# A convolution feeding a multiplicative FFN: loading x in two halves, issuing row transposes as soon as their rows are stored, and transposing block 2 on TensorE

## The chip, the cores and the metric

The kernel runs on one core of a Trainium2 chip. The metric is the device time of one launch in microseconds. The kernel before took 584.01, 588.37 and 587.26 us in three runs, median 587.26. One execution was profiled: it took 585.55 us, and its span, from the first to the last instruction of the program, is 583.8 us. Durations below are from that execution.

## The reference

What is computed, cut to what matters:

```
x: (8, 3904, 192) float32      weight: (8 heads, 7 taps)
w1, w2: (192, 1024)   w3: (1024, 1024)   w_out: (1024, 192)

w   = softmax(weight, axis=-1)
# causal convolution over the sequence; head h owns channels 24h .. 24h+23
c[b, s, h, :] = sum_k w[h, k] * x[b, s - 6 + k, h, :]        (zeros before s = 0)
c   = c.reshape(31232, 192)
out = ((c @ w1) * (c @ w2)) @ w3 @ w_out
```

## The kernel before

The 31232 tokens are two halves of TS = 15616 tokens (NS = 2, the index r). Both halves are worked on together: each takes 64 of the 128 partitions. Everything after the convolution goes in rounds R = 0 to 30 of CH = 512 tokens of each half (the last has 256).

**Convolution.** The tokens are cut into windows of 58 (64 rows of x, the first 6 of them overlap). Windows come in blocks of sizes 10, 10, 10, 30, 32 and then five times 36 (`SIZES`, L52); block b starts at token `tok(FIRST[b])`, which is 0, 580, 1160, 1740, 3480, 5296, 7384, 9432, 11520, 13568. `load_x` (L91) loads a block's x into one or two `xb` tiles (two halves of the block's windows, `halves_of`) with POOL's DMA queue, converting to bf16. There are six `xb` buffers. `conv` (L231) multiplies the windows with a band matrix made of the weights, head by head, into PSUM, and copies the result to the tile `convo` (two buffers). `store` (L262) writes `convo` with SP's DMA queue to a DRAM tensor `rows`, one row per token.

**Transposition.** `first_product` needs channels on partitions. `xT` is a ring of 2048 tokens (four rounds), in three parts of 128 partitions. `transposes(R)` (L301) fills a round of it with three DMA transposes from `rows`, on SP's queue. `pe_transposes(b)` (L286) does it without DRAM: 15 transposes on TensorE from `convo` into PSUM, and three copies into `xT`, two on DVE and one on ACT. In the kernel before, blocks 0 and 1 take that way; block 2 goes through `rows`, with the last windows of block 1 (`store(1, 19)`, from token 1102).

**The products.** `first_product(R)` (L327) runs eight steps `ft`; each has 12 matmuls for `pa` and `pb`, ACT's copy of `pa` to `asb` and DVE's product into `abT`. `second_product(R, r)` (L352) multiplies `abT` with `W_sb` = w3 @ w_out; ACT copies the result to `osb` and SP's queue stores it. It lags two rounds (`LAG`). PSUM is four tiles of two banks, shared by all of these.

**Order.** It is written out by hand (`manual_schedule`): every engine does its instructions in the order in which the code issues them.

- POOL's opening: x of block 0, the masks (L152), four DMAs of `load_first` (L133), the identity (L158, L159), the loads of `wn[0]` and the two halves of `wn[2]` (L163 to L165), the products of half of the band matrix (L203, `band_taps(1, ...)`), then `wn[1]` (L407), and blocks 1 and 2 of x. DVE makes the other half of the products at the same time as POOL's earlier work, sums them into `Aband` (L211), and copies it to the other partitions (L214).
- Rounds 0, 1 and 2 of `first_product` have the convolutions of blocks 1, 2 and 3 between their steps (L433 to L443); in round 1 after step 0: the rest of block 2's convolution, its store, and `transposes(2, 1152)`. After round 2's step 5: block 3's store, `transposes(3)` and `transposes(4)`. Then comes w3 @ w_out on TensorE.
- The loop over R (L462) does, in each round: `first_product(R)` (from R = 3), `second_product(R - 2)` for both halves, `conv` of one to three heads of the next block by the table `plan`, `store` of a block after its last head, and `transposes(R + 2)` last. Block 4 is stored in round 4, block 5 in round 7, block 6 in 11, block 7 in 15, block 8 in 19, block 9 in 23. In the round of a block's first head, `load_x` of the next block is issued whole (L473); the DMA waits until the convolution that read the buffers before is done.

So SP's queue holds, in this order, the outputs of round R - 2, a block's store if there is one, and the transposes for round R + 2.

Of the kernel before, what the change touches and what calls it, by code (L numbers as in the profile page):

```python
# [10 lines left out]
BF16 = mybir.dt.bfloat16  # L11
# [6 lines left out]
def kernel(  # L18
# [10 lines left out]
    nc = tc.nc  # L29
# [6 lines left out]
    PAD = K - 1  # L36

    NS = 2
    TS = B * S // NS
    CH = 512  # L40
    NR = -(-TS // CH)
    RING = 4 * CH
    LAG = 2
    Q = 64
    ST = Q - PAD
# [4 lines left out]
    SIZES = [10, 10, 10, 30, 32] + [36] * 5  # L50
    assert sum(SIZES) == NWIN
    NB = len(SIZES)  # L52
    FIRST = [sum(SIZES[:b]) for b in range(NB)]
# [4 lines left out]
    def tok(i):  # L58
        return (i // WB) * S + (i % WB) * ST

    const = ctx.enter_context(tc.tile_pool(name="const", bufs=1))
# [12 lines left out]
    def slot(shape, dtype, name):  # L74
        return stage.tile(shape, dtype, tag="slot", bufs=5, name=name)
# [4 lines left out]
    def halves_of(b):  # L80
        n = SIZES[b] // 2
        return [(FIRST[b], 2 * n)] if 2 * n <= MAXN else [(FIRST[b], n), (FIRST[b] + n, n)]

    x_rows = x.rearrange("b s d -> (b s) d")
    xb_of, zero_rows = {}, {}

    def x_spans(r, i, m):
        return bass.AP(tensor=x.tensor, offset=(r * TS + tok(i) - PAD) * D,
                       ap=[[D, Q], [ST * D, m], [1, D]])

    def load_x(b):  # L91
        tiles = []
        zeros_of = zero_rows[b] = []
        for i0, n in halves_of(b):
            xb = work.tile([128, n, D], BF16, tag="xb", bufs=6, name="xb")
            w = 0
            if i0 == 0:
                nc.gpsimd.memset(xb[:, 0, :], 0.0)
                for r in range(NS):
                    nc.gpsimd.dma_start(out=xb[Q * r:Q * r + Q, 1:n, :], in_=x_spans(r, 1, n - 1))  # L100
                w = n
            while w < n:
                i = i0 + w
                m = min(n - w, WB - i % WB)
                at_end = i + m == NWIN
                if at_end:
                    m -= 1
                if m:
                    for r in range(NS):
                        nc.gpsimd.dma_start(out=xb[Q * r:Q * r + Q, w:w + m, :],  # L110
                                            in_=x_spans(r, i, m))
                if i % WB == 0:
                    zeros_of += [(xb, 0, w), (xb, 1, w)]
                w += m
                if at_end:
                    nc.gpsimd.memset(xb[Q:128, w, :], 0.0)
                    t = tok(NWIN - 1) - PAD
                    nc.gpsimd.dma_start(out=xb[0:Q, w, :], in_=x_rows[t:t + Q, :])
                    nc.gpsimd.dma_start(out=xb[Q:Q + PAD + LAST, w, :],
                                        in_=x_rows[TS + t:TS + t + PAD + LAST, :])  # L120
                    w += 1
            tiles.append(xb)
        if len(tiles) == 1:
            xb_of[b] = [(tiles[0], 0), (tiles[0], SIZES[b] // 2)]
        else:
            xb_of[b] = [(tiles[0], 0), (tiles[1], 0)]


    def load_first():
        xb = xb_of[0][0][0]  # L130
        for r in range(NS):
            for p0, p1 in ((PAD, PAD + 48), (PAD + 48, Q)):
                nc.gpsimd.dma_start(  # L133
                    out=xb[Q * r + p0:Q * r + p1, 0, :],
                    in_=x_rows[r * TS + p0 - PAD:r * TS + p1 - PAD, :])

    wall = const.tile([128, H, K], FP32)
    nc.scalar.dma_start(out=wall, in_=weight.partition_broadcast(128))
    load_x(0)

    tiny = const.tile([128, 1], FP32)
# [9 lines left out]
    for m, base in ((cmask, 0), (lmask, -Q)):  # L151
        nc.gpsimd.affine_select(  # L152
            out=m, in_=ones.unsqueeze(2).to_broadcast([128, K, Q]),
# [1 line left out]
            fill=0.0, base=base, channel_multiplier=1)  # L155
    nc.vector.tensor_copy(out=cmask[Q:128], in_=lmask[Q:128])
    load_first()
    ident = const.tile([128, 128], BF16)  # L158
    make_identity(nc, ident)  # L159

    wn = [const.tile([128, DFF], BF16, name=f"wn{k}", tag=f"wn{k}") for k in range(3)]
    wsw = [const.tile([128, DFF], BF16, name=f"ws{k}", tag=f"ws{k}") for k in range(3)]
    nc.gpsimd.dma_start(out=wn[0], in_=moe_w1[0:128, :])  # L163
    nc.gpsimd.dma_start(out=wn[2][0:Q], in_=moe_w1[128:192, :])
    nc.gpsimd.dma_start(out=wn[2][Q:128], in_=moe_w2[128:192, :])  # L165

    def warm(n):
        t = banks("warm")
# [11 lines left out]
        out=wall, in0=wall, in1=wmax.unsqueeze(2).to_broadcast([128, H, K]), op=ALU.subtract)  # L180
# [3 lines left out]
    for r in range(NS):  # L184
        ps = slice(Q * r, Q * r + Q)
        nc.vector.tensor_tensor(
            out=wsb[ps],
# [13 lines left out]
    def band_taps(g, engine):  # L201
        cprod_of[g] = slot([128, 2, K, Q], FP32, "cprod")
        engine.tensor_tensor(  # L203
            out=cprod_of[g],
            in0=cmask.unsqueeze(1).to_broadcast([128, 2, K, Q]),
            in1=wsb[:, g].unsqueeze(3).to_broadcast([128, 2, K, Q]),
            op=ALU.mult)
# [23 lines left out]
    def conv(b, h0, nh, evict=None):  # L231
# [27 lines left out]
        if h0 + nh == H:  # L259
            del xb_of[b]  # L260

    def store(b, first=0):  # L262
        n = SIZES[b] // 2
        convo = convo_of[b]
        for c in range(2):
            w = 0
            while w < n:
                i = FIRST[b] + c * n + w
                if i < first:
                    w += 1  # L270
                    continue
                left = WB - 1 - i % WB
                src = convo[Q * c:Q * c + ST, w:w + max(1, min(n - w, left))]
                src = src.rearrange("s w k r g -> s w (k r g)")
                j0 = tok(i)
                if left == 0:
                    nc.sync.dma_start(out=rows[j0:j0 + LAST, :], in_=src[0:LAST, 0, :])
                    w += 1
                    continue
                m = min(n - w, left)  # L280
                dst = rows[j0:j0 + ST * m, :].rearrange("(w s) c -> s w c", s=ST)
                for s0, s1 in ((0, 48), (48, ST)):
                    nc.sync.dma_start(out=dst[s0:s1], in_=src[s0:s1])
                w += m
# [16 lines left out]
    def transposes(R, first=0):  # L301
        t0, t1 = max(R * CH, first), min((R + 1) * CH, TS)
        a = t0 % RING
        for k in range(NP):
            nc.sync.dma_start_transpose(  # L305
                out=xT[k][:, a:a + t1 - t0], in_=rows[t0:t1, k * 128:(k + 1) * 128])
# [78 lines left out]
    def w3_transpose(jt):  # L385
        w3b = w3b_of.pop(jt)
        tps = banks_bf16("w3ps")
        for gt in range(JT):
            nc.tensor.transpose(out=tps[:, gt, :], in_=w3b[:, gt * 128:(gt + 1) * 128],  # L389
                                identity=ident)  # L390
        w3T_of[jt] = stage.tile([128, JT, 128], BF16, tag="w3T", bufs=3, name="w3T")
        nc.vector.tensor_copy(out=w3T_of[jt], in_=tps[:, 0:JT, :])  # L392
# [11 lines left out]

    band_taps(0, nc.vector)
    band_taps(1, nc.gpsimd)
    nc.gpsimd.dma_start(out=wn[1], in_=moe_w2[0:128, :])  # L407
    for b in (1, 2):
        load_x(b)
    band_sum(0)  # L410
# [8 lines left out]
    for k in (0, 2, 1):  # L419
        swap_w(k, 1, (P, A))  # L420
    load_x(3)
    load_wo()
    for jt in range(JT):
# [3 lines left out]
    def seq(*fs):  # L427
        def run():
            for f, *a in fs:
                f(*a)  # L430
        return run

    first_product(0, {  # L433
        3: seq((conv, 1, 0, 4)),
        5: seq((conv, 1, 4, 4)),
        7: seq((pe_transposes, 1), (store, 1, 19), (conv, 2, 0, 4))})
    first_product(1, {
        0: seq((conv, 2, 4, 4), (store, 2), (transposes, 2, 1152)),
        7: seq((conv, 3, 0, 1), (conv, 3, 1, 1))})
    first_product(2, {  # L440
        1: seq((conv, 3, 2, 1), (conv, 3, 3, 1)),
        3: seq((conv, 3, 4, 1), (conv, 3, 5, 1)),
        5: seq((conv, 3, 6, 1), (conv, 3, 7, 1), (store, 3), (transposes, 3), (transposes, 4))})  # L443

    w3_transpose(0)
    w3_transpose(1)
# [7 lines left out]
    R = LAG  # L454
    for b in range(PROLOGUE_BLOCKS, NB):
        last = tok(FIRST[b]) // CH - (2 if b == PROLOGUE_BLOCKS else 3)
        hs, n = list(range(H)), last - R + 1
        for j in range(n):
            plan[R + j] = [(b, hs.pop(0)) for _ in range(-(-len(hs) // (n - j)))]
        R = last + 1  # L460

    for R in range(LAG, NR + LAG):  # L462
        if LAG < R < NR:
            first_product(R)
        for r in range(NS):
            second_product(R - LAG, r)
        heads = plan.get(R, [])
        if heads and heads[0][1] == 0:
            b = heads[0][0]
            for xb, r, w in zero_rows.pop(b):  # L470
                nc.gpsimd.memset(xb[Q * r:Q * r + PAD, w, :], 0.0)
            if b + 1 < NB:
                load_x(b + 1)  # L473
        for j, (b, h) in enumerate(heads):
            conv(b, h, 1, (V,) if j < 2 else (A,))
        if heads and heads[-1][1] == H - 1:
            store(b)
        if LAG < R < NR - 2:
            transposes(R + 2)


# [28 lines left out]
```

## Time and profile before

| what | us |
|---|---|
| median of three runs (584.01 to 588.37) | 587.26 |
| the profiled execution | 585.55 |
| its span | 583.8 |
| TensorE (PE) busy | 535.8 (92%) |
| VectorE (DVE) busy | 358.4 (61%) |
| ScalarE (ACT) busy | 319.6 (55%) |
| GpSimd (POOL) busy | 50.1 (9%) |
| DMA packets of SP's queue, share of 16 engines' span | 35.0% |
| DMA packets of POOL's queue, share of 16 engines' span | 24.8% |

The busy time of PE counts a matmul longer when TensorE's clock is granted at half speed, so a busy PE isn't PE at its best. How the clock stands is shown by the granted clock, and by the time of six matmuls of `first_product`, which is 0.65 us at the full clock and 1.28 us at half. "SPq" and "POOLq" are the DMA queues of SP and POOL: a time there is that of issuing, not of the transfer.

### The profile page before, as it was taken

The page shows a single profiled execution, that of the slowest core. Times are in us where ns is not written, and L with a number is a line of the kernel's source. Part 1 is how long each engine was busy: PE and PEld are TensorE (multiplying, and loading weights), DVE is VectorE, ACT ScalarE, POOL GpSimd, SP SyncE. Part 2 cuts the span into 40 slices and gives each one's busy share as a digit, 9 for nine tenths or more (in the row PEclk, how much of TensorE's full clock was granted, in tenths as well). Part 3 has the DMA queues.
Part 4 walks back from the last instruction along what each step waited for, and adds up shares of the span by engine and source line. Part 5 has one row for each costly group of instructions (what it writes and reads, how often), then busy time and mean ns, then how long its engine had stood idle before and what let it go on. Part 6 is the DMA issues. An engine that isn't in the chain of part 4 may idle for free.

```text
span 583.8 us, 12613 instructions
## 1 busy us (share of the span) xinstructions
PE 535.8 (92%) x5425; PEld 343.8 (59%) x5425; DVE 358.4 (61%) x330; ACT 319.6 (55%) x360; POOL 50.1 (9%) x80
## 2 busy tenths in 40 slices
PE   6894888996999689997899989999999999999997
PEld 2441484664566446665366666656666666666687
DVE  6671636664666466665566666876666666666550
ACT  2872735653565255553455545666555556666642
POOL 9632300020003000030000000000000000000000
PEclk8996998999899989999799999999999999999999
DMA  6999995459346953349533272235532262333214
GB/s 92 182 215 177 113 169 93 82 107 195 79 83 124 180 92 82 82 83 204 106 83 83 77 170 42 70 82 147 125 83 64 62 155 75 82 82 83 69 56 136
DMA packets 131830, 63.72 MB, mean 109 GB/s; under 512 B 84620, under 2 KB 130366, under 8 KB 131774
## 3 DMA queue, kind: packets, MB, share of 16 engines
q1 hardware_dynamic: 93470, 46.26, 35.0%
q0 software_dynamic: 38160, 16.63, 24.8%
q8 instruction: 42, 0.69, 0.5%
q14 instruction: 14, 0.11, 0.1%
q10 hardware_dynamic: 144, 0.03, 0.0%
HBM read 33.28 MB, written 35.13 MB: 117 GB/s over the span
## 4 chain that ended last, share of the span: by engine, by line
PE 80%; DMA 12%; ACT 3%; POOL 2%; DVE 2%; SPq 1%; issue 1%; ACTq 0%; POOLq 0%
PE pa L340 27%; PE pb L340 27%; PE ops L358 25%; DMA xT<-rows 10%; PE cps L247 1%; ACT asb L346 1%; DMA rows<-convo 1%; DVE abT L347 1%; DMA wn<-in_moe_w_dram 1%; SPq L305 1%; ACT convo L257 0%; POOL xb L133 0%; ACT osb L363 0%; POOL xb L100 0%; ACT ws L319 0%
## 5 line engine op out<-in xcount | busy, mean ns | idle before, releaser
L347 DVE TENSOR_TENSOR abT<-asb,pb 128x1024 bf16<-128x1024 bf16 (+1 forms) x248 | 298.0, 1203 | 106.4 <-ACT asb L346 51.8
L346 ACT CAST asb<-pa 128x1024 bf16<-128x1024 f32 (+1 forms) x248 | 247.5, 999 | 112.4 <-PE pa L340 111.7
L340 PE MATMUL pa<-xT,wn 64*128 64x512 bf16 (+1 forms) x744 | 206.6, 381 | 24.2 <-DMA xT<-rows 21.5
L340 PE MATMUL pa<-xT,ws 64*128 64x512 bf16 (+1 forms) x744 | 206.7, 381 | 11.3 <-DMA xT<-rows 10.6
L340 PEld LDWEIGHTS <-wn 64*128 64x128 bf16 x1488 | 138.8, 95 | 119.9 <-issue 26.3
L340 PE MATMUL pb<-xT,wn 64*128 64x512 bf16 (+1 forms) x744 | 206.2, 380 | 0.7 <-DVE abT L347 0.7
L340 PE MATMUL pb<-xT,ws 64*128 64x512 bf16 (+1 forms) x744 | 199.8, 381 | 0.0
L340 PEld LDWEIGHTS <-ws 64*128 64x128 bf16 x1488 | 130.9, 95 | 82.0 <-issue 19.3
L358 PEld LDWEIGHTS <-abT 128*128 128x128 bf16 x1952 | 159.6, 98 | 11.7 <-issue 11.7
L358 PE MATMUL ops<-W_sb,abT 128*128 128x192 bf16 x1952 | 166.1, 246 | 0.0
L363 ACT COPY osb<-ops 128x768 f32<-128x768 f32 (+1 forms) x62 | 48.9, 789 | 127.6 <-PE ops L358 127.6
L257 DVE CAST convo<-cps 128x864 bf16<-128x864 f32 (+4 forms) x53 | 44.9, 894 | 93.2 <-PE cps L247 80.7
L110 POOL DMA_DIRECT2D xb<-in_x_dram x38 | 29.9, 809 | 175.6 <-issue 103.1
L247 PE MATMUL cps<-xb,Aband 64*64 64x432 bf16 (+3 forms) x320 | 18.9, 322 | 5.2 <-DVE Aband L211 2.9
L257 ACT CAST convo<-cps 128x640 bf16<-128x640 f32 (+8 forms) x29 | 15.3, 581 | 3.5 <-PE cps L247 2.9
L247 PEld LDWEIGHTS <-Aband 64*64 64x64 bf16 x320 | 6.4, 110 | 14.5 <-issue 8.2
L398 PE MATMUL wps<-wo_b,w3T 128*128 128x192 bf16 x64 | 6.6, 246 | 1.3 <-DVE w3T L392 1.2
L170 PE MATMUL warm<-zeros 128*128 128x512 bf16 x19 | 6.5, 507 | 1.3 <-DVE zeros L144 1.3
L392 DVE COPY w3T<-w3ps 128x1024 bf16<-128x1024 bf16 x8 | 5.4, 689 | 2.9 <-PE w3ps L389 2.9
L400 ACT CAST W_sb<-wps 128x192 bf16<-128x192 f32 x8 | 2.6, 320 | 8.1 <-PE wps L398 8.1
L398 PEld LDWEIGHTS <-w3T 128*128 128x128 bf16 x64 | 5.1, 98 | 1.7 <-DVE w3T L392 1.7
L383 POOL DMA_DIRECT2D w3b<-in_moe_w_dram x8 | 4.3, 558 | 7.9 <-DMA xb<-in_x_dram 6.7
(47 smaller groups left out, 50.8 us busy)
## 6 DMA issues: line engine op xcount, KB each, us to landing
out_dram<-osb SPq DMA_DIRECT2D x60, 384.0 KB
xb<-in_x_dram POOLq DMA_DIRECT2D x14, 432.0 KB, 12.6
rows<-convo SPq DMA_DIRECT2D x7, 648.0 KB
w3b<-in_moe_w_dram POOLq DMA_DIRECT2D x8, 256.0 KB, 12.3
xb<-in_x_dram POOLq DMA_DIRECT2D x6, 240.0 KB, 7.2
xb<-in_x_dram POOLq DMA_DIRECT2D x4, 360.0 KB, 9.3
xT<-rows SPq DMA_TRANSPOSE x87
xb<-in_x_dram POOLq DMA_DIRECT2D x6, 192.0 KB, 10.3
```

The source lines that it names most:

```text
L110: nc.gpsimd.dma_start(out=xb[Q * r:Q * r + Q, w:w + m, :], in_=x_spans(r, i, m))
L170: nc.tensor.matmul(t[:, j % 2, :], zeros[:, 0:128], zeros, start=True, stop=True)
L247: nc.tensor.matmul(view(slice(Q * c, Q * c + Q), r)[:, :, j * G:(j + 1) * G], band_of(h, r), xb[Q * r:Q * r + Q, w0:w0 + n, h * G:(h + 1) ...
L257: f[e % len(f)](out=dst, in_=src[:, :, :, o:o + m])
L305: nc.sync.dma_start_transpose(out=xT[k][:, a:a + t1 - t0], in_=rows[t0:t1, k * 128:(k + 1) * 128])
L340: nc.tensor.matmul(p[:, r, 0:N], w_of(i, k, r)[rs, ft * 128:(ft + 1) * 128], xT[k][rs, r0:r0 + N], start=(k == 0), stop=(k == NP - 1))
L346: nc.scalar.copy(out=asb[:, :, 0:N], in_=pa[:, :, 0:N])
L347: nc.vector.tensor_tensor(out=ab[:, ft, :, 0:N], in0=asb[:, :, 0:N], in1=pb[:, :, 0:N], op=ALU.mult)
L358: nc.tensor.matmul(ops[:, g // 2, (g % 2) * D:(g % 2) * D + D], ab[:, jt, r, g * 128:(g + 1) * 128], W_sb[:, jt, :], start=(jt == 0), stop ...
L363: nc.scalar.copy(out=osb.rearrange("p (a g) d -> p a (g d)", g=2), in_=ops[:, 0:ng // 2, 0:2 * D])
L392: nc.vector.tensor_copy(out=w3T_of[jt], in_=tps[:, 0:JT, :])
L398: nc.tensor.matmul(wps[:, 0, 0:D], w3T[:, gt, :], wo_b[:, gt, :], start=(gt == 0), stop=(gt == JT - 1))
```

## The change

1. `load_x` takes the halves that it is to load. In the loop, half 0 of the next block is issued in the round of a block's first heads, half 1 in the round after. In the opening both are loaded as before.
2. `transposes` in the loop are issued as far as rows are stored (`stored`), up to three rounds ahead (`sent`): `transposes(5)` in round 2, 6 and 7 in round 4 behind the store of block 4, 8 in round 5, and from there `transposes(R + 3)` in round R.
3. Block 2 is transposed on TensorE, after step 2 of round 1. Of its rows only windows 26 to 29 are stored (`transposes(3)` needs them), and `store(1, 19)` and `transposes(2, 1152)` are gone.
4. POOL's first work: `load_first` is two DMAs of 58 partitions, where it was four of 48 and 10. The identity and the loads of `wn[2]` come after POOL's products for the band matrix, in the order `wn[2]` (two DMAs), `wn[1]`, identity.

```diff
-    def load_x(b):
-        tiles = []
-        zeros_of = zero_rows[b] = []
-        for i0, n in halves_of(b):
+    def load_x(b, parts=(0, 1)):
+        tiles = xb_of.setdefault(b, [])
+        zeros_of = zero_rows.setdefault(b, [])
+        for i0, n in [v for e, v in enumerate(halves_of(b)) if e in parts]:
...
-            for p0, p1 in ((PAD, PAD + 48), (PAD + 48, Q)):
-                nc.gpsimd.dma_start(
-                    out=xb[Q * r + p0:Q * r + p1, 0, :],
-                    in_=x_rows[r * TS + p0 - PAD:r * TS + p1 - PAD, :])
+            nc.gpsimd.dma_start(out=xb[Q * r + PAD:Q * r + Q, 0, :],
+                                in_=x_rows[r * TS:r * TS + ST, :])
...
     load_first()
-    ident = const.tile([128, 128], BF16)
-    make_identity(nc, ident)
...
     nc.gpsimd.dma_start(out=wn[0], in_=moe_w1[0:128, :])
-    nc.gpsimd.dma_start(out=wn[2][0:Q], in_=moe_w1[128:192, :])
-    nc.gpsimd.dma_start(out=wn[2][Q:128], in_=moe_w2[128:192, :])
...
+    stored, sent = [0], [3]
+
     def store(b, first=0):
+        stored[0] = tok(FIRST[b] + SIZES[b]) if b + 1 < NB else TS
...
     band_taps(1, nc.gpsimd)
+    nc.gpsimd.dma_start(out=wn[2][0:Q], in_=moe_w1[128:192, :])
+    nc.gpsimd.dma_start(out=wn[2][Q:128], in_=moe_w2[128:192, :])
     nc.gpsimd.dma_start(out=wn[1], in_=moe_w2[0:128, :])
+    ident = const.tile([128, 128], BF16)
+    make_identity(nc, ident)
...
-        7: seq((pe_transposes, 1), (store, 1, 19), (conv, 2, 0, 4))})
+        7: seq((pe_transposes, 1), (conv, 2, 0, 4))})
     first_product(1, {
-        0: seq((conv, 2, 4, 4), (store, 2), (transposes, 2, 1152)),
+        0: seq((conv, 2, 4, 4)),
+        2: seq((pe_transposes, 2), (store, 2, 26)),
...
+    sent[0] = 5
...
+    done_of = {}
     for R in range(LAG, NR + LAG):
...
-        if heads and heads[0][1] == 0:
-            b = heads[0][0]
-            for xb, r, w in zero_rows.pop(b):
+        if heads:
+            b, h = heads[0]
+            for xb, r, w in zero_rows.pop(b, []):
                 nc.gpsimd.memset(xb[Q * r:Q * r + PAD, w, :], 0.0)
-            if b + 1 < NB:
-                load_x(b + 1)
+            done_of[b] = done_of.get(b, -1) + 1
+            if b + 1 < NB and done_of[b] < 2:
+                load_x(b + 1, (done_of[b],))
...
-        if LAG < R < NR - 2:
-            transposes(R + 2)
+        while sent[0] < NR and sent[0] <= R + 3 and min((sent[0] + 1) * CH, TS) <= stored[0]:
+            transposes(sent[0])
+            sent[0] += 1
```

## The prediction, made before the result was known

> **What bounds the kernel now.** I read the page first: busy times and the slices. PE is busy 92% of the span, and its busy share dips in the 4th, 10th, 14th and 19th slice of 14.6 us, each time with a lower granted clock in that slice or the next.
>
> ```profile
> PE   6894888996999689997899989999999999999997
> PEclk8996998999899989999799999999999999999999
> ```
>
> So PE is the bound, and the question is what stops it. Second, the waits of PE, where one line holds nearly everything after the opening:
>
> ```profile
> PE pa L340 <- DMA xT<-rows: 32.1, 13, 6.6
> ```
>
> Third, the chain of waits (start, length, what), for where these are and what one costs. From one start of `ops` to the next is one round:
>
> ```profile
> 134.50 2.76 PE ops L358 x32
> 137.37 9.35 DMA xT<-rows
> ...
> 158.92 5.40 PE ops L358 x64
> ...
> 192.15 3.01 PE ops L358 x36
> 195.16 10.73 DMA xT<-rows
> ...
> 217.84 5.39 PE ops L358 x64
> ...
> 234.32 5.39 PE ops L358 x64
> ...
> 267.22 1.45 PE ops L358 x17
> 268.67 11.20 DMA xT<-rows
> ...
> 292.33 5.39 PE ops L358 x64
> ```
>
> The reader sees an undisturbed round of 234.32 - 217.84 = 16.48 us, and rounds of 24.42, 25.69 and 25.11 us in which a transpose came late. This price holds the wait and the cold clock after it. Two later rounds are a little long: starts 341.70 to 359.78 and 409.15 to 426.25, 18.08 and 17.10 us. Fourth, the timeline of PE at round 3 (start, length, what, idle before), and PE's granted clock by stretches after round 2's stall:
>
> ```profile
> 87.86 0.37 PE L340 MATMUL pa<-xT,ws 64*128 64x512 bf16 x1 [1.71 <-DMA xT<-rows]
> 89.69 0.58 PE L340 MATMUL pa<-xT,wn 64*128 64x512 bf16 x1 [1.44 <-DMA xT<-rows]
> ```
>
> ```profile
> 50.60:58.10 7.50, 5.63 (x28) 0.50 1.99 170
> ```
>
> The last columns are length, PE busy, granted clock (0.50), DMA share, GB/s. Fifth, the queues at round 11, where a transpose that needs no new rows stands behind a store, beside a load:
>
> ```profile
> 257.21 3.44 POOL L110 DMA_DIRECT2D xb<-in_x_dram  x4 [58.55 <-issue]
> ```
>
> ```profile
> 258.60 0.80 SPq L283 DMA_DIRECT2D rows<-convo  x2
> ...
> 264.53 8.24 SPq L305 DMA_TRANSPOSE xT<-rows  x3
> ```
>
> And the opening:
>
> ```profile
> 6.39 1.09 DVE L203 TENSOR_TENSOR cprod<-cmask,wsb 128x896 f32<-128x896 bf16 x1
> 9.23 1.80 DVE L214 COPY Aband<-Aband 64x128 bf16<-64x128 bf16 x1
> ```
>
> ```profile
> 3.22 0.60 POOL L152 TENSOR_SCALAR_AFFINE_SELECT cmask<-ones 128x448 bf16<-128x448 bf16 x1
> 6.81 0.82 POOL masks.py:199 TENSOR_SCALAR_AFFINE_SELECT ident<-ident 128x128 bf16<-128x128 bf16 x1
> 9.21 1.75 POOL L203 TENSOR_TENSOR cprod<-cmask,wsb 128x896 f32<-128x896 bf16 x1
> ```
>
> **The change part by part.** The sum is made against the profiled execution, 585.55 us (span 583.8 and 1.75 around it), which is 1.7 below the median.
>
> *Transposes ahead.* In the kernel before, `transposes(9)`, (13), (17) and (21) need only rows stored one block earlier, yet stand behind the stores of blocks 5 to 8 in the same round, with one round of cover. Now each goes out a round before that store, and what stands behind the store is 10, 14, 18, 22, needed three rounds later. Store to landed transpose takes 20 to 25 us by the chain (183.5 to 205.9 for block 5), against two full rounds of cover, 33 us. So these stalls go whole: 25.69 - 16.48 = 9.2, 25.11 - 16.48 = 8.6, 18.08 - 16.48 = 1.6, 17.10 - 16.48 = 0.6; together -20.0. Late next in these rounds is nothing that I find: the neighbours run at 16.41 to 16.49. Each moved transposition is three DMAs of about 1.2 us of SP's issue time, moved past the two outputs of the round between; in round 4 the next outputs stand behind `transposes(7)` too. SP waits 279.1 us in all for `osb`, so that cover is ample, and five `osb` buffers carry an output that leaves a few us late. The ring slot of round R + 3 is that of R - 1, which PE has left, so SP doesn't gain a wait.
>
> *Round 6.* `transposes(6)` needs rows of block 4, stored in round 4 in both kernels. Its order (store, then transposes) and the load beside it stay. Its stall of 24.42 - 16.8 = 7.6 (16.80 is the round from 101.39 to 118.19, with the same three heads of convolution) stays: 0, between -7.6 if the store is quicker and +2 if what now follows it disturbs.
>
> *Halves of x, one per round.* I cost it at 0. Both halves wait for buffers that the same last head of an earlier block releases, one matmul group apart; POOL has nothing between them that takes time. In the trace POOL runs rounds ahead of its program order: the x load at 257.21 is block 9's, written in round 16, and it starts with round 11, as soon as block 6's convolution is done. So the loads still start together beside each store. Bounds: 0, or the gain of a real spreading, which is rival A.
>
> *Block 2 on TensorE.* Round 2's stall goes: waits of 6.55 and 1.84, and a cold stretch in which 5.63 us of PE's work would take half, 2.8; -11.2. Added on PE: 15 transposes; the 30 of blocks 0 and 1 were busy 2.7, so +1.35. Their three copies (DVE 0.46 twice, ACT 0.64) lie beside matmuls; `xT` is read five steps later. Round 2 had its convolutions of block 3 partly under the cold clock; at the full clock ACT has eight `asb` copies of 1.0 and some eight evictions of 0.77, 14 us, against 13 of PE: +1.0, between 0 and 2.
>
> *Round 3.* The stall stays: `transposes(3)` needs block 3's store, and from its last convolution to `first_product(3)` lie the same two steps, w3's product and one `second_product`. Before, it waited 1.71 and 1.44, and went cold for about 3.4 us (six matmuls at 1.28), 1.7 lost. Now everything up to here comes 11 us earlier, so block 5's x (landed until about 64 us before) runs beside the store and block 6's after it. Before, block 6's load already ran beside it nearly throughout: I take +1.0, between -2 and, if DMA work alone sets the time, +10 (rival B).
>
> *The opening.* DVE's copy took 1.80 us beside POOL's product, and 0.19 at 12.78 without it; the product moves forward, so up to 1.6 goes, and `wn[1]` leaves up to 1.6 earlier. But POOL's product now starts with DVE's own product. POOL's 128-wide select took 0.82 beside that product, longer than the 0.60 of a 448-wide one alone, and ended just after it (7.63 against 7.48): one waits for the other. If POOL waits, its product ends near 9.2, `wn[2]` and `wn[1]` are issued until 11.0 (before 11.49), the identity comes at 12, when PE wants it: -0.5. If DVE waits its 1.75, Aband is ready no sooner than before: 0. The DMA of 58 partitions: 18 KB landed in 2.4 us and 3.8 KB in 2.2, so its 24 KB in some 2.5, or, if fewer engines carry it, up to 2.8 more, which is 0.5 late on the first convolution. I take -0.5, between -1.6 and +0.6.
>
> The Trainium skill, "SBUF — State Buffer", section "Who interferes with whom", says that a DVE instruction with two SBUF inputs contends with a GpSimd instruction that reads SBUF, and that the later one blocks for the whole of the other. The select's row agrees; by the rule alone this part would bring 0 to 0.5, not 1.6. The skill's "DMA: Bandwidth & Descriptors", section "Why a DMA increments its semaphore by 16 and not by 1", speaks against this change: a DMA runs on the largest number of engines up to 16 that divides its slowest dimension, so 58 partitions get two where 48 got 16. No row here shows a 58-row load; by the rule the first convolution could come later.
>
> Sum: -20.0 + 0 + 0 - 11.2 + 1.35 + 1.0 + 1.0 - 0.5 = -28.35; 585.55 - 28.35 = 557.2. I predict 557.
>
> **The rivals.**
>
> A. The halves do spread the x load, and store and transposes have the DMA engines to themselves. For: PE's waits for transposes at rounds 2, 6, 9 and 13 stand beside x loads. Against: the buffers' release starts both halves. Then rounds 3 and 6 lose their stalls too, 7.6 and 4.9 + 1: 557 - 13 = 544.
>
> B. DMA work binds the first 90 us. For: 215 GB/s in the slice at 29 to 44 us, 177 in the next, and a share above 1.5 of the engines from 44 to 64; the work up to round 3 is nearly the same and gets 11 us less. Against: the share falls to 0.21 from 91 on, and the x of block 5 isn't wanted until round 5. Then round 3 gives ten back: 567.
>
> C. One round more of cover isn't enough, and rounds 10 and 14 stall as 9 and 13 did. Against: 33 us of cover for 25. Then 557 + 17.8 = 575.
>
> D. Slower. SP's queue becomes the bound: transposes stand two deep behind a store that waits for its rows, and outputs behind both; with five `osb` buffers, two an output round, SP may stand about 33 us before ACT, then PE's PSUM tiles, stop. It decides from there. To end slower than before, the six stores would have to stop PE by 29 us in all, 5 each, so SP would stand some 38 us at each. For: at round 11 SP is at it from 258.60 to 281.7, 23 us. Against: PE's longest wait for `osb` is 0.3. Then about 593.
>
> **How the numbers follow.** The likeliest (0.58) is 557, its own range 551 to 564 from the bounds of rounds 2, 3 and the opening and the 4.4 us between runs. A has 0.10, B 0.20, C 0.06, D 0.04; 0.02 is left for no change within 1%. The range is 547 to 568: it takes in B and part of A's side, and leaves out A's lower half, C and D, under 0.2. About 1% (5.9 us) is what a measurement of this kernel can tell from no change. Faster: 0.58 + 0.10 + 0.20 + 0.06 = 0.94; same 0.02; slower 0.04.
>
> **What would show it.** Right: no wait of PE for `xT<-rows` at rounds 2, 9 and 13, and rounds of about 16.5 us from round 7 to the end; one wait left at round 3 and one at round 6 with a cold clock behind; POOL's two halves issued within 4 us of each other when a block's last convolution ends. Wrong: a round 3 with ten us of waiting (B), no wait at round 6 (A), a wait at round 10 or 14 (C), PE waiting for `osb` (D). If DVE's or POOL's product in the opening takes over 2 us, one waited for the other.

## The result, and the profile after

The changed kernel takes 557.36 us, the median of four runs (555.71 to 558.18), against 587.82 (584.01 to 590.27) for the kernel before: a ratio of 0.9484, 95% interval 0.9427 to 0.9541. Its profiled execution took 556.73 us, with a span of 555.0 us; 28.8 us less than before's span.

The page's slices, PE's busy share and its granted clock:

```profile
PE   6889879996999999999999999999999999999996
PEclk9899999998899999999999999999999999999999
```

After the 11th slice (153 us) both rows stand at 9 until the last; before, the dips went on to the 20th. The waits of PE, in us, times and the longest:

```profile
PE pa L335 <- DMA xT<-rows: 9.1, 6, 2.6
```

Of the 32.1 us of waiting for transposes 9.1 are left, and the timeline of PE says where (start, length, what, idle before): three at round 3, three at round 6.

```profile
76.57 0.39 PE L335 MATMUL pa<-xT,wn 64*128 64x512 bf16 x1 [0.71 <-DMA xT<-rows]
78.90 0.37 PE L335 MATMUL pa<-xT,ws 64*128 64x512 bf16 x1 [1.95 <-DMA xT<-rows]
80.22 0.37 PE L335 MATMUL pa<-xT,wn 64*128 64x512 bf16 x1 [0.92 <-DMA xT<-rows]
...
133.82 0.39 PE L335 MATMUL pa<-xT,wn 64*128 64x512 bf16 x1 [2.64 <-DMA xT<-rows]
136.37 0.58 PE L335 MATMUL pa<-xT,ws 64*128 64x512 bf16 x1 [2.16 <-DMA xT<-rows]
137.68 0.58 PE L335 MATMUL pa<-xT,wn 64*128 64x512 bf16 x1 [0.70 <-DMA xT<-rows]
```

The chain of waits shows the rounds, from one start of `ops` to the next:

```profile
125.12 2.65 PE ops L353 x31
127.77 9.87 DMA xT<-rows
...
149.94 5.40 PE ops L353 x64
...
183.16 5.39 PE ops L353 x64
199.65 5.39 PE ops L353 x64
```

The round that ends with round 6's products is 149.94 - 125.12 = 24.82 us, as long as it was (24.42). Round 9's, 25.69 before, is 199.65 - 183.16 = 16.49 now. Round 13's, 25.11 before, is 16.49 too by the same rows further on, and none after it up to round 29 is over 16.5.

POOL's x loads, the lines that ask whether the two halves came apart:

```profile
56.80 4.48 POOL L110 DMA_DIRECT2D xb<-in_x_dram  x6 [7.08 <-PE cps L239]
...
115.19 3.39 POOL L110 DMA_DIRECT2D xb<-in_x_dram  x4 [43.66 <-issue]
172.92 4.52 POOL L110 DMA_DIRECT2D xb<-in_x_dram  x6 [54.34 <-PE cps L239]
```

They didn't: both halves of block 6 leave at 56.80, of block 7 at 115.19, of block 8 at 172.92, each in one go. SP's stores start at 57.44, 116.39 and 174.54, beside them; of block 4, with the transposes of rounds 6 and 7 behind it:

```profile
116.39 0.82 SPq L278 DMA_DIRECT2D rows<-convo  x2
...
122.40 13.85 SPq L300 DMA_TRANSPOSE xT<-rows  x6
```

And the opening, DVE and then POOL:

```profile
9.23 0.34 DVE L206 COPY Aband<-Aband 64x128 bf16<-64x128 bf16 x1
...
14.62 0.29 DVE L314 COPY ws<-wn 64x512 bf16<-64x512 bf16 x1 [1.59 <-DMA wn<-in_moe_w_dram]
```

```profile
6.52 2.51 POOL L195 TENSOR_TENSOR cprod<-cmask,wsb 128x896 f32<-128x896 bf16 x1 [0.51 <-DVE wsb L178]
```

POOL's product takes 2.51 us where it took 1.75, because DVE's product runs beside it until 7.48: started after that, it takes 1.75 again (the kernel with the weights first, below). DVE's copy is down from 1.80 to 0.34. DVE still waits 1.59 us for `wn[1]`.

### The profile page after: what moved, and what is told of

Read it like the earlier page. It is cut to its first block, busy times and chain, and to the rows that moved or that the text cites. A ratio compares the mean times of both kernels' runs of the same rounds, so it can differ in the third digit from the quotient of the medians.

```text
span 555.0 us, 12621 instructions
## 1 busy us (share of the span) xinstructions
PE 530.1 (96%) x5440; PEld 342.6 (62%) x5440; DVE 357.3 (64%) x332; ACT 319.9 (58%) x361; POOL 49.2 (9%) x78
## 4 chain that ended last, share of the span: by engine, by line
PE 87%; DMA 5%; DVE 3%; ACT 3%; POOL 1%; issue 1%; ACTq 0%; POOLq 0%
PE pa L335 28%; PE ops L353 28%; PE pb L335 28%; DMA xT<-rows 4%; DVE abT L342 2%; ACT asb L341 2%; PE cps L239 2%; DMA wn<-in_moe_w_dram 1%; PE wps L393 1%; PE w3ps L384 0%; ACT osb L358 0%; POOL xb L100 0%; DVE xT L294 0%; POOL cprod L195 0%; ACT xT L294 0%
## 5 line engine op out<-in xcount | busy, mean ns | idle before, releaser
L335 PE MATMUL pa<-xT,wn 64*128 64x512 bf16 (+1 forms) x744 | 202.1, 377 | 8.2 <-DMA xT<-rows 5.0
L335 PE MATMUL pa<-xT,ws 64*128 64x512 bf16 (+1 forms) x744 | 202.2, 377 | 4.7 <-DMA xT<-rows 4.1
L335 PE MATMUL pb<-xT,wn 64*128 64x512 bf16 (+1 forms) x744 | 204.0, 377 | 0.8 <-DVE abT L342 0.4
L162 PEld LDWEIGHTS <-zeros 128*128 128x128 bf16 x19 | 2.2, 125 | 4.7 <-issue 2.7
```

What stands on the lines that cost most here:

```text
L162: nc.tensor.matmul(t[:, j % 2, :], zeros[:, 0:128], zeros, start=True, stop=True)
L335: nc.tensor.matmul(p[:, r, 0:N], w_of(i, k, r)[rs, ft * 128:(ft + 1) * 128], xT[k][rs, r0:r0 + N], start=(k == 0), stop=(k == NP - 1))
```

## The experiments

All times are medians; the kernel before was run beside each group, and its median there is given.

**Parts of the change alone.** Kernel before at 588.33 us for this and the next three.

*Transposes ahead only*: the kernel before, with

```diff
-        if LAG < R < NR - 2:
-            transposes(R + 2)
+        while sent[0] < NR and sent[0] <= R + 3 and min((sent[0] + 1) * CH, TS) <= stored[0]:
+            transposes(sent[0])
+            sent[0] += 1
```

> The kernel before, with the transposes in the loop issued up to three rounds ahead, and nothing else of the change. My theory: the stalls of rounds 9, 13, 17 and 21 go whole, 20.0 us, and the waits of rounds 2, 3 and 6 stay as they are in the kernel before (11.2, 4.9 and 7.6): 587.8 - 20.0 = 568 against the median of before. Rival: the rounds were relieved by the halves of x as well, and with whole loads one round more of cover isn't enough, so rounds 10 and 14 stall: 575 to 586.

Measured: 566.75 (565.8 to 569.68), ratio 0.9653 (0.9622 to 0.9683). The rounds of 9, 13, 17 and 21 are 16.5 us each; those of 3 and 6 keep their waits. So these 20 us are the transposes' alone, with whole loads.

*Block 2 on TensorE only*: the kernel before, with

```diff
-        7: seq((pe_transposes, 1), (store, 1, 19), (conv, 2, 0, 4))})
+        7: seq((pe_transposes, 1), (conv, 2, 0, 4))})
     first_product(1, {
-        0: seq((conv, 2, 4, 4), (store, 2), (transposes, 2, 1152)),
+        0: seq((conv, 2, 4, 4)),
+        2: seq((pe_transposes, 2), (store, 2, 26)),
```

> The kernel before, with block 2 transposed on PE after step 2 of round 1 (and only its windows 26 to 29 stored), and nothing else of the change. My theory: round 2's stall of 11.2 goes, 1.9 come back in round 1, some 0.4 in rounds 3 and 6: 587.8 - 9 = 579. Rival: the DMA work of the first 90 us sets the time, and round 3 waits for what round 2 no longer does: 585 to 588.

Measured: 577.33 (577.13 to 577.56), ratio 0.9824 (0.9809 to 0.984): 11.0 less. Round 3's waits are 1.23 and 2.17 (1.71 and 1.44 before), so the DMA work of the opening doesn't take the gain back. 21.6 and 11.0 make 32.6; the whole change brings 30.5. The opening was put in neither, and isn't what is missing (below); 32.6 lies within the interval of the whole change, 27.0 to 33.7 us.

*The changed kernel with whole loads*:

```diff
-            if b + 1 < NB and done_of[b] < 2:
-                load_x(b + 1, (done_of[b],))
+            if b + 1 < NB and done_of[b] == 0:
+                load_x(b + 1)
```

> The changed kernel, with the x of a block loaded whole in the round of its predecessor's first heads, as in the kernel before. My theory: splitting the load moves nothing, since the two halves wait for buffers that the same heads release; the time is that of the changed kernel, 557.4 within 2 us, and POOL's x loads start at the same places, in one go. Rival: the split thins the collision, and without it rounds 3 and 6 wait longer and rounds 10 and 14 stall: 560 to 575.

Measured: 558.39 (557.19 to 559.47), ratio 0.9501 (0.948 to 0.9523), that of the changed kernel within both intervals. The loads stand in POOL's timeline as before:

```profile
58.64 4.48 POOL L110 DMA_DIRECT2D xb<-in_x_dram  x6 [8.62 <-PE cps L239]
```

The split alone does nothing.

**What holds up rounds 3 and 6.** *The halves made to wait*: in the changed kernel, POOL copies a column of a round's `abT` ahead of the DMAs, so that they can't leave before.

```diff
+    gate = const.tile([128, 1], BF16, name="gate", tag="gate")
+    loads_of = {2: [(5, 0)], 3: [(5, 1), (6, 0)], 4: [(6, 1)], 6: [(7, 0)], 7: [(7, 1)],
+                9: [(8, 0)], 10: [(8, 1)], 13: [(9, 0)], 14: [(9, 1)]}
...
             first_product(R)
+        for j, (b, part) in enumerate(loads_of.get(R, [])):
+            nc.gpsimd.tensor_copy(out=gate, in_=abT_of[R][:, 4 * j, 0, 0:1])
+            load_x(b, (part,))
...
-            done_of[b] = done_of.get(b, -1) + 1
-            if b + 1 < NB and done_of[b] < 2:
-                load_x(b + 1, (done_of[b],))
```

> The changed kernel, with each half of x made to wait on POOL for a product of first_product in a chosen round (a copy of one column of abT stands before its DMAs): block 5 in rounds 2 and 3, block 6 in 3 and 4, block 7 in 6 and 7, block 8 in 9 and 10, block 9 in 13 and 14, so that no x load but the end of block 5's first half runs beside the store and the transposes before rounds 3 and 6. My theory: the remaining stalls of rounds 3 and 6 are the collision with the x load; both go or nearly go, 5.3 and 8.0 us: 557.4 - 12 = 545, within 3. Rival: store, landing and transposes take their 20 us by themselves (issue on SP's queue, and the row packets); both stalls stay: 557.

Measured: 544.42 (543.77 to 544.84), ratio 0.9267 (0.9248 to 0.9285), 13 less than the changed kernel, and 14 less than the one with whole loads, which ran beside it. PE has no wait for `xT<-rows` left, and the chain of waits has round 6 at 137.03 - 120.21 = 16.82 us (24.82 in the changed kernel) and round 3 at 16.7 in the same way (22.1):

```profile
120.21 5.40 PE ops L353 x64
...
137.03 5.40 PE ops L353 x64
```

POOL's timeline shows the first half of block 7, which left at 115.19 beside the store, leaving after round 6 has begun; the second half leaves at 147.49:

```profile
129.79 0.19 POOL L470 COPY gate<-abT 128x1 bf16<-128x1 bf16 x1 [30.96 <-DVE abT L342]
130.31 1.70 POOL L110 DMA_DIRECT2D xb<-in_x_dram  x2 [0.33 <-PE pa L335]
```

SP's timeline has block 4's store and the transposes of rounds 6 and 7 behind it:

```profile
111.48 0.83 SPq L278 DMA_DIRECT2D rows<-convo  x2
...
116.28 10.77 SPq L300 DMA_TRANSPOSE xT<-rows  x6
```

So the last two stalls were the x load beside store and transposes, not the length of these by themselves. With the load, the way from block 4's store to the last transpose of round 6 took 137.68 - 116.39 = 21.3 us; without it nobody waited for these transposes when round 6 began at 126.48, so the way took 15 us at most.

**Was it the store, the cover, or the load?** Kernel before at 586.73 us for the next four.

*Transposes before the store of the same round*, not a round earlier; the kernel before, with

```diff
+        early = R != 4
+        if early and LAG < R < NR - 2:
+            transposes(R + 2)
         if heads and heads[-1][1] == H - 1:
             store(b)
-        if LAG < R < NR - 2:
+        if not early:
             transposes(R + 2)
```

> The kernel before, with transposes(R + 2) ahead of the store of the same round on SP's queue (but in round 4, where they need it); not a round earlier. It parts two readings of the gain at rounds 9 and 13: standing behind the store, or one round more of cover. My theory: the store is what delayed them; three transposes issued ahead of it land within the round of cover though x is loaded beside them, and the 20.0 go: 588 - 20 = 568, as with the transposes issued a round ahead. Rival: the x load beside them is enough to make them late, and rounds 9 and 13 keep some of their stalls: 573 to 585.

Measured: 567.84 (565.88 to 568.4), ratio 0.9674 (0.9645 to 0.9703), the time of the kernel with the transposes a round ahead. Round 9 shows how: in the kernel before, the transposes for it are issued behind the store of block 5, with an x load beside them (POOL's line first, then SP's), and PE waits 4.31 and 3.00 us for them.

```profile
181.91 4.52 POOL L110 DMA_DIRECT2D xb<-in_x_dram  x6 [53.95 <-PE cps L247]
```

```profile
183.53 7.06 SPq L283 DMA_DIRECT2D rows<-convo  x4
190.68 8.20 SPq L305 DMA_TRANSPOSE xT<-rows  x3
```

With the transposes in front the load is still there, and PE doesn't wait; the round takes 16.49 us:

```profile
184.68 4.52 POOL L110 DMA_DIRECT2D xb<-in_x_dram  x6 [54.64 <-PE cps L247]
```

```profile
185.22 4.41 SPq L305 DMA_TRANSPOSE xT<-rows  x3
189.72 8.60 SPq L283 DMA_DIRECT2D rows<-convo  x4
```

Three transposes that stand in front of the store on SP's queue land in time with the x load beside them; behind it they don't. It is the place behind the store that cost the 20 us, and a round more of cover is one way out of it.

*The kernel before with the x loads made to wait*: the same waits as above, at the same rounds. Of the change it has only that `load_x` can take one half, since the waits are set half by half.

> The kernel before, with nothing of the change but x loads that wait on POOL for first_product of chosen rounds, as in the gated kernel. It asks whether the transposes ahead were needed at all. My theory: what makes a transpose late is the x load beside store and transposes, so with one round of cover only and the old order rounds 3, 6, 9, 13, 17 and 21 lose their stalls (4.9, 7.6, 9.2, 8.6, 1.6, 0.6), and round 2 keeps its 11.2: 588 - 32.5 = 555.5. Rival: behind a store one round of cover is too little in any case, and rounds 9 and 13 keep most of their 17.8: 570 to 575.

Measured: 552.91 (551.27 to 553.55), ratio 0.9421 (0.9393 to 0.9449): 33.8 less, more than the whole change. What is left of PE's waits is round 2, but for 0.2 us later on:

```profile
PE pa L339 <- DMA xT<-rows: 8.4, 4, 6.5
```

The transposes of rounds 9 and 13 still stand behind a store here, with one round of cover, and don't come late; these are SP's lines for round 9:

```profile
170.74 5.76 SPq L282 DMA_DIRECT2D rows<-convo  x4
176.60 7.39 SPq L304 DMA_TRANSPOSE xT<-rows  x3
```

So the stalls of rounds 9 and 13, 17.8 of the 20.0 us, needed both: the place behind the store, and the load beside it. For rounds 17 and 21, 1.6 and 0.6 us, the load's part isn't shown. In the kernel before their stores stand at 333.08 and 400.53, and POOL's last x load is issued at 261.36, so no load ran beside them; here, with as little beside them, the rounds take 16.50 and 16.68 us. What made them late before stays open.

**The opening.** *The changed kernel with the opening of the kernel before*: `load_first` in four DMAs, identity and `wn[2]` ahead of POOL's product.

> The changed kernel with the opening of the kernel before (four DMAs in load_first, identity and wn[2] ahead of POOL's product). My theory: the opening was worth 0 to 0.8 us, since its end is set by the landing of wn[1], which came 14.6 to 15.5 in three runs of the new opening and 15.1 in the old; the time is 557.4 to 558.4. Rival: the product's move is worth the 1.5 us by which DVE's copy got shorter: 559.

Measured: 558.2 (554.79 to 559.55), ratio 0.9504 (0.9474 to 0.9535). Not to be told from 557.36. DVE's copy is back at 1.79 and the wait for `wn[1]` is 1.25.

*The gated kernel with the weights first*:

```diff
     nc.gpsimd.dma_start(out=wn[0], in_=moe_w1[0:128, :])
+    nc.gpsimd.dma_start(out=wn[2][0:Q], in_=moe_w1[128:192, :])
+    nc.gpsimd.dma_start(out=wn[2][Q:128], in_=moe_w2[128:192, :])
+    nc.gpsimd.dma_start(out=wn[1], in_=moe_w2[0:128, :])
...
     band_taps(1, nc.gpsimd)
-    nc.gpsimd.dma_start(out=wn[2][0:Q], in_=moe_w1[128:192, :])
-    nc.gpsimd.dma_start(out=wn[2][Q:128], in_=moe_w2[128:192, :])
-    nc.gpsimd.dma_start(out=wn[1], in_=moe_w2[0:128, :])
```

> The gated kernel, with the loads of wn[2] and wn[1] issued right behind wn[0], before POOL's product, which then starts when DVE's is over. My theory: wn[1] sets the end of the opening; issued 2.4 us sooner it lands near 12.5, DVE's last copy of it no longer waits 2.3, and POOL's product takes 1.75 instead of 2.51; first_product(0) starts near 14, and the time is 1 to 2 below the gated kernel's 544.4: 543. Rival: the loads share the DMA engines and land when they land, or the cold clock falls on the first round instead: 544.4, no change.

Measured: 542.8 (542.02 to 544.02), ratio 0.9253 (0.9229 to 0.9277); the gated kernel, in another group of runs, took 544.42 (543.77 to 544.84). POOL's product is short again and DVE's last weight copies follow each other without a wait:

```profile
7.62 1.75 POOL L198 TENSOR_TENSOR cprod<-cmask,wsb 128x896 f32<-128x896 bf16 x1
```

```profile
12.63 0.57 DVE L317 COPY ws<-wn 64x512 bf16<-64x512 bf16 x2
```

`first_product(0)` starts at 14.49, for 15.93 in the gated kernel.

**Both once more, side by side, without the transposes ahead.** Kernel before at 587.78 us. The gated kernel again:

> The gated kernel once more, on one chip with the kernel that follows, so that the 1.6 us that the early weights seemed to bring can be told from the difference of chips. My theory: 544.4, within 1.

and the kernel with weights first, its transposes as in the kernel before:

```diff
-        while sent[0] < NR and sent[0] <= R + 3 and min((sent[0] + 1) * CH, TS) <= stored[0]:
-            transposes(sent[0])
-            sent[0] += 1
+        if LAG < R < NR - 2:
+            transposes(R + 2)
```

> The gated kernel with the weights loaded first, and with transposes(R + 2) in round R as in the kernel before, not up to three rounds ahead. My theory: with the x loads out of the way one round of cover is enough, so the transposes ahead bring nothing now, and the early weights bring 1.5: 543, below the gated kernel beside it. Rival 1: the transposes ahead still save something at rounds 9 and 13: 545 to 550. Rival 2: the early weights bring nothing that can be measured: 544.4.

Measured: 544.28 (543.9 to 545.36), ratio 0.9256 (0.9225 to 0.9286), and 542.62 (541.7 to 543.23), ratio 0.9221 (0.919 to 0.9251). The runs of the two don't overlap. They differ in two things, early weights and no transposes ahead, and the two together bring some 1.7 us. That these are the early weights' rests on the kernel with the weights first above, which has early weights and transposes ahead: 542.8, though not run beside this pair. With the loads out of the way the transposes ahead bring nothing that can be seen: the rounds of the second kernel are 16.3 to 16.8 us up to round 7 and at most 16.5 from there to round 29, and PE waits for no transpose. The two kernels with early weights are the fastest, some 15 below the changed kernel.

## Why the prediction was right, point by point

Forecast was 557, and measured is 557.36. That it agrees so closely is in part luck: the runs of the changed kernel lie 2.5 us apart, and the sum of -28.35 was taken from an execution of the kernel before at 585.55, while the medians, 587.82 and 557.36, differ by 30.5. From the two profiled traces, the steps (predicted, measured):

- *Transposes ahead*: -20.0, and the rounds of 9, 13, 17 and 21 are 9.2, 8.6, 1.6 and 0.6 shorter, -20.0. The part alone brings 21.6 between medians. The place behind the store was rightly named, and it is one half of the mechanism. The prediction took the 20 to 25 us from store to landed transpose as given; in rounds 9 and 13 the other half was the x load beside the store, without which the old order doesn't stall (16.49 us each in the kernel before with the loads made to wait).
- *Round 6*: 0, measured 24.82 - 24.42 = +0.4.
- *Halves of x*: 0, measured 0 by the kernel with whole loads, 558.39. Rival A had the right price for a real spreading, 13 us: the gated kernel is 13.0 below the changed one. It was the change that didn't do it.
- *Block 2 on TensorE*: -11.2 + 1.35 + 1.0 = -8.85. In the traces -11.4 + 1.9 = -9.5; the part alone brings 11.0 between medians. It fell elsewhere than I put it: round 2 shows the whole 11.4 (13.41 us on PE's timeline from its last convolution before to its last matmul, where it was 24.78), and the cost is in round 1, 12.05 for 10.14, +1.9. ACT didn't bind round 2; PE waits there for `abT` only, 0.2 to 0.3 us at each of three steps with convolutions. So the term of 1.0 for ACT in round 2 was wrong, the 15 transposes were busy 1.0 us and not 1.35, and 0.9 of waits and delay around them in round 1 were missed. That these nearly make up for each other is luck.
- *Round 3*: +1.0, measured +0.25: from where PE was ready, 85.48 before and 75.85 after, to the next `ops` it takes 15.91 and 16.16. Rival B is out: the load ran beside the store before, and runs beside it still; coming earlier didn't add.
- *The opening*: -0.5 between -1.6 and +0.6, measured -0.2. POOL waited for DVE, as one of the two readings had it; `first_product(0)` starts at 15.33 for 16.14, -0.8. By round 1's first step, at 33.68 for 33.86, only 0.2 is left, since the clock at the start of round 0 was lower in this execution (length, PE busy, granted clock; before and after):

```profile
16.10:22.90 6.80, 5.94 (x52) 1.00 1.53 178
```

```profile
15.30:22.70 7.40, 7.09 (x52) 0.77 1.56 186
```

The prediction hadn't this: it priced the opening to the start of round 0. Nor do the traces tie the lower clock to the opening. In six profiled executions with the old opening round 1's first step starts between 33.86 and 35.60, in four with the changed one between 33.68 and 35.57; the granted clock over the first 6.8 us of round 0 lies between 0.56 and 1.00 in the six, and between 0.56 and 0.75 in the four. So the 0.2 is far less than the same opening varies by. The time of the kernel with the old opening, 558.2, agrees with next to nothing.

The terms as measured in the traces: -20.0 + 0.4 + 0 - 11.4 + 1.9 + 0.25 - 0.2 = -29.05, beside a span 28.8 shorter. Rival C is out by the rounds of 10 and 14, 16.48 us both, and D by PE's waits for `osb`, 0.5 us in all.

The Trainium skill's rule on a shared port ("SBUF — State Buffer", section "Who interferes with whom") agrees with POOL's product at 2.51 us beside DVE's and 1.75 without it. Waiting for the whole of DVE's product it would have ended at 7.48 + 1.75 = 9.23; it ended at 6.52 + 2.51 = 9.03. What I drew from "DMA: Bandwidth & Descriptors" against the change, two engines for 58 partitions, shows nowhere in the time: the two loads of 58 partitions (21.8 KB each, not 24) landed 2.3 and 2.7 us after issue, the four before 1.9 to 2.8, and the first convolution waited for `Aband` and not for them. The same section names an exception on trn2, by which some copies from GpSimd's queue are spread over 16 engines whatever divides their partitions; the prediction left it out, and which of the two holds for this load no run shows. Nor does any run show the 2.8 us more that the prediction allowed for fewer engines.

## What to carry to other kernels

A transfer issued ahead on a queue is let go by its wait and not by its place in the program: to spread loads over rounds, give them a wait that belongs to the round (here a one-column copy of that round's product), and look in the trace where they start. When a transfer comes late, ask what stands ahead of it on its queue and what runs beside it: nearly all of the same 20 us went by taking it out from behind the store, or by moving the load that ran beside the store. And price an early gain to the end of the next long stretch, over several executions: here round 1 started up to 1.9 us apart in executions of one opening, more than the 0.8 us that one pair of traces showed at the start of round 0.

## What the runs showed of the hardware

- POOL's and SP's queues are separate, but with an x load on the one the other's way from store to landed transpose, at round 6, took 21.3 us; without the load it took 15 at most.
- The opening varies between executions. With the changed opening, `first_product(0)` started between 15.33 and 16.23 in four executions, and DVE's copy that waits for `wn[1]` between 14.62 and 15.53. With the old one, `first_product(0)` started between 16.14 and 16.48 in six.
